# Gradient operands made inside the last attention, and all output chunks behind it in two-bank tiles

## The chip, the cores and the metric

The kernel runs on one core of one Trainium2 chip. The metric is the device time of one execution in microseconds (us); the span, which the profile uses, runs from the first to the last instruction and is about 2 us shorter.

Words used below. *PE* does the matrix products, *VectorE* (DVE), *ScalarE* (ACT) and *GpSimd* (POOL) work on elements, *SyncE* (SP) issues most DMAs. A matrix product lands in *PSUM*, where this kernel's tiles take one bank (512 columns) or two (1024); to *evacuate* is to copy PSUM into on-chip memory, from where this kernel's DMAs write it out. A *block* is a DMA of 512 KB. In the code cuts, `T` transposes a chunk of `wo`, `M` multiplies with it, and `Z` says how many zero blocks each stage gets.

## The reference

Two attention layers and two MLP layers share one set of weights (A, B, A, B) and run on a single token; the result is the output and the gradients of all inputs:

```python
x = x + A(layernorm(x)); x = x + B(layernorm(x))
x = x + A(layernorm(x)); x = x + B(layernorm(x))
out, vjp = jax.vjp(f, A_x, A_k_cache, A_v_cache, A_wq, A_wo, B_w1, B_b1, B_w2)
return (out, *vjp(grad_out))
```

A token's weight gradient is an outer product of two short vectors, but it is as large as the weight. The gradients of the K and V caches are zero except in the last 4096 of 32768 positions, so most of them is plain zeros: 112 blocks that the kernel may write at any time, and uses to keep the DMA engines busy.

## The kernel before

The backward pass ends with the attention of the first layer, called A1. Its first step multiplies the gradient with `wo`. Nine of `wo`'s 16 chunks are kept on the chip; seven (9 to 15) are loaded again into a ring of six buffers. So six loads can be issued early, and the seventh waits until the first buffer is free.

```python
def zeros(n):                       # on SyncE's queue
    for _ in range(min(n, len(zero_jobs))):
        nc.sync.dma_start(zero_jobs.pop(0), zt[:])
def bg_zeros(n, after):             # on GpSimd's queue, not before `after` is made
    ...
def attn_bwd(...):
    held = {}
    for c in range(NR, min(NO, NR + NB)):        # chunks 9..14
        held[c] = wo_load(c)                     # nc.sync.dma_start
    bg_zeros(Z["A3c" if first else "A1c"], g_bf) # 6 zero blocks
    ...
    def T(i):
        c = late[i]
        if c not in held:
            held[c] = wo_load(c)                 # chunk 15
        ...                                      # transpose, reduce
    pipe(list(range(len(late))), T, M)
    ...
    else:
        zeros(Z["A1d"])                          # 26 zero blocks
    # --- cut: do, rows_mm with V, softmax backward, dq, product with wq;
    #     six chunks of the w2 gradient are made in between (run(..)) ---
```

Everything after the pipeline of T and M needs all seven chunks. SyncE issued its DMAs in program order here: below, the zeros begin at 304.14 us, only after the seventh load, which had waited for its buffer until 303.7.

Behind the attention the remaining gradient chunks are made. A chunk takes four 512-column products; `out_banks` gives four one-bank tiles or, once the pool "pair" exists, two two-bank tiles:

```python
def out_banks():
    if "pair" in pools:
        ts = [pools["pair"].tile([P, 1024], FP32, ...) for _ in range(2)]
        ...
    bs = [psum1([P, 512], FP32, "ops") for _ in range(4)]
# --- cut ---
g0, g0b = attn_bwd(g1, g1b, "A1", sA1, False, "X0")
# --- cut: gradient row operands are made here, after the attention ---
run(1000)                                        # rest of the w2 gradient
dw_wide(lambda: R["w1"], 256, F // 2, True, out_6)
run(4)
pt.release()
pools["pair"] = ctx.enter_context(...)           # two-bank tiles from here on
```

## Time and profile before

| | before |
|---|---|
| time, median of 4 runs | 462.57 us (460.12 to 464.96) |
| profiled span | 458.9 us |
| bytes moved by DMA | 172.24 MB |
| DMA rate when it is full | 417 to 419 GB/s |

At 417 GB/s the bytes alone take 413 of the 459 us, so the kernel is for the most part bound by DMA, and what can be won is stretches in which DMA is not full. The page shows them over the whole span in 40 slices (DMA in tenths of busy time, then GB/s):

```profile
span 458.9 us, 11945 instructions
...
DMA  8999999988999999999998999999995889799997
GB/s 322 387 411 414 406 408 342 410 307 316 416 417 370 390 342 351 411 414 416 416 414 326 311 336 368 359 412 418 416 418 235 354 321 400 309 413 402 418 411 303
```

The low slices after the 30th belong to the end of the last attention and what follows. Stage by stage (stretch, its length, then busy time and instructions of PE, weight load, DVE, ACT and POOL, the share of PE's clock that was granted, the DMA share, GB/s):

```profile
core 0: us, PE busy (x) PEld busy (x) DVE busy (x) ACT busy (x) POOL busy (x), PEclk, DMA share, GB/s
345.00:350.00 5.00, 1.59 (x10) 1.02 (x11) 1.83 (x9) 0.00 (x0) 2.02 (x10) 0.50 0.81 330
350.00:355.00 5.00, 4.40 (x40) 3.77 (x38) 3.92 (x15) 2.02 (x2) 4.47 (x22) 0.50 0.25 99
360.00:365.00 5.00, 3.94 (x16) 0.77 (x13) 3.43 (x6) 3.95 (x8) 0.00 (x0) 0.50 0.69 281
375.00:380.00 5.00, 3.10 (x20) 0.70 (x20) 4.12 (x5) 4.22 (x5) 0.00 (x0) 0.50 0.71 285
390.00:395.00 5.00, 4.66 (x42) 1.33 (x40) 5.00 (x6) 4.70 (x5) 0.00 (x0) 0.70 0.43 166
400.00:440.00 40.00, 32.88 (x192) 8.51 (x192) 38.62 (x35) 37.58 (x41) 0.00 (x0) 0.50 1.02 412
```

Three holes: the row operands (345 to 355), the one-bank chunks (360 to 380), and the K blocks, where a 1 MB write needs four chunks (390 to 395). With two-bank tiles (from 400) DMA is full.

SyncE's queue in the last attention (issue time, duration of the group, what, count):

```profile
289.07 15.01 SPq L336 DMA_DIRECT2D wo_c<-in_A_wo_dram  x7
304.14 31.08 SPq L130 DMA_DIRECT2D out_dram<-zt  x26
335.32 22.52 SPq L974 DMA_DIRECT2D out_dram<-wo_b  x7
```

All seven loads come first, then 26 zeros, which take SyncE 31 us, then outputs. The chain of work that ended last (start, duration, what) shows what the seventh load meant:

```profile
303.32 0.37 PE acc L223 x8
303.76 6.69 DMA wo_c<-in_A_wo_dram
310.50 0.64 PE tps L187 x8
```

PE freed the buffer at 303.7 us, and PE went on as soon as the load landed, at 310.5. The price of a one-bank and a two-bank evacuation (group, count | busy, mean ns of one | idle before):

```profile
L146 DVE CAST K<-ops 128x1024 bf16<-128x1024 f32 x15 | 17.7, 1221 | 0.9 <-PE ops L223 0.6
L149 ACT CAST K<-ops 128x1024 bf16<-128x1024 f32 x17 | 17.0, 1012 | 1.7 <-PE ops L223 1.2
...
L146 DVE CAST so<-ops 128x512 bf16<-128x512 f32 x4 | 2.7, 689 | 1.1 <-PE ops L223 1.0
...
L149 ACT CAST so<-ops 128x512 bf16<-128x512 f32 x4 | 2.3, 586 | 0.4 <-PE ops L223 0.4
```

Twice 689 is 1378 ns against 1221, twice 586 is 1172 against 1012: each instruction carries about 160 ns that do not depend on its size.

### The profile page before, as it was taken

What the parts mean: (1) busy time and instruction counts of PE and PEld (TensorE: products, weight loads), DVE (VectorE), ACT (ScalarE), POOL (GpSimd) and SP (SyncE); (2) the same over time, 40 slices, a digit from 0 to 9 for tenths busy, and PEclk for the clock granted to TensorE, in tenths of its full rate; (3) what the DMA queues carried; (4) which work ended last, traced back from release to release, by engine and by line L of the source; (5) the groups of instructions that cost most, each with busy time, mean ns of one, the idle gap of its engine ahead of it and who ended that gap; (6) DMA issues with size and microseconds to landing.
All of it is one profiled execution on the core that took longest, in us unless ns stands there. A gap on an engine that the chain in (4) does not pass through costs nothing.

```text
span 458.9 us, 11945 instructions
## 1 busy us (share of the span) xinstructions
PE 328.7 (72%) x5080; PEld 225.6 (49%) x5080; DVE 246.9 (54%) x519; ACT 219.3 (48%) x268; POOL 61.5 (13%) x159
## 2 busy tenths in 40 slices
PE   0565755577996998877997889775885676779730
PEld 0333434566466997854895779643534111222100
DVE  3124101376332776663265755564555779999960
ACT  1122100165242886773581655351031689998940
POOL 2000000002422214142330020112006000000000
PEclk9989555596777999895697769987565555755555
DMA  8999999988999999999998999999995889799997
GB/s 322 387 411 414 406 408 342 410 307 316 416 417 370 390 342 351 411 414 416 416 414 326 311 336 368 359 412 418 416 418 235 354 321 400 309 413 402 418 411 303
DMA packets 52257, 172.24 MB, mean 375 GB/s; under 512 B 5200, under 2 KB 12396, under 8 KB 51180
## 3 DMA queue, kind: packets, MB, share of 16 engines
q1 hardware_dynamic: 39680, 126.37, 71.3%
q0 software_dynamic: 12480, 45.11, 24.5%
q8 instruction: 39, 0.64, 0.5%
q14 instruction: 14, 0.11, 0.1%
q10 hardware_dynamic: 44, 0.01, 0.0%
HBM read 72.89 MB, written 98.58 MB: 374 GB/s over the span
## 4 chain that ended last, share of the span: by engine, by line
PE 21%; issue 9%; DVE 8%; ACT 8%; DMA 7%; POOL 1%; DVEq 0%; ACTq 0%; SPq 0%; POOLq 0%
PE tps L187 6%; PE ops L223 5%; DMA w_c<-in_B_w_dram 4%; PE acc L223 4%; ACT wo_b L149 3%; DVE wq_b L146 3%; DMA wo_c<-in_A_wo_dram 3%; DVE K L146 3%; ACT st_o L149 2%; PE d L223 2%; PE tps L602 1%; PE sm L223 1%; PE rw L887 1%; ACT wo_c L149 1%; ACT w_c L603 1%
## 5 line engine op out<-in xcount | busy, mean ns | idle before, releaser
L139 POOL DMA_DIRECT2D out_dram<-zt x86 | 45.7, 535 | 43.3 <-DMA out_dram<-zt 40.7
L223 PEld LDWEIGHTS <-w_c 128*128 128x128 bf16 x1120 | 36.3, 102 | 20.9 <-DMA w_c<-in_B_w_dram 13.9
L603 ACT COPY w_c<-tps 128x1024 bf16<-128x1024 bf16 x28 | 28.3, 1012 | 25.5 <-PE tps L602 24.8
L146 DVE CAST wo_b<-ops 128x512 bf16<-128x512 f32 (+3 forms) x40 | 33.2, 878 | 9.2 <-PE ops L223 8.9
L605 DVE CUSTOM_DVE_ANT_0 scr<-w_c,gbc 128x1024 bf16<-128x1024 bf16 x28 | 34.2, 1221 | 7.2 <-DMA w_c<-in_B_w_dram 5.2
L149 ACT CAST wo_b<-ops 128x512 bf16<-128x512 f32 (+2 forms) x34 | 27.0, 870 | 16.4 <-PE ops L223 16.4
L149 ACT COPY K<-tps 128x1024 bf16<-128x1024 bf16 x19 | 18.7, 1019 | 30.9 <-PE tps L187 30.9
L223 PE MATMUL q<-wq_b,nA_pair 128*32 128x512 bf16 x128 | 14.0, 541 | 16.6 <-DMA wq_b<-in_A_wq_dram 15.1
L770 DVE CUSTOM_DVE_ANT_0 wo_c<-wo_c,gbc 128x1024 bf16<-128x1024 bf16 x14 | 16.3, 1218 | 12.4 <-DMA wo_c<-in_A_wo_dram 10.4
L602 PE MATMUL tps<-ident_bf,w_c 128*128 128x128 bf16 x224 | 22.7, 263 | 0.0
L146 DVE COPY K<-tps 128x1024 bf16<-128x1024 bf16 x13 | 8.8, 689 | 24.9 <-PE tps L187 24.9
L149 ACT COPY w_b<-tps 128x1024 bf16<-128x1024 bf16 x20 | 19.5, 1015 | 5.3 <-PE tps L187 5.2
L187 PE MATMUL tps<-ident_bf,K 128*128 128x128 bf16 x256 | 21.7, 249 | 0.0
L223 PE MATMUL ops<-Tw 2*128 2x512 bf16 x56 | 15.9, 560 | 6.5 <-ACT wo_b L149 4.1
L187 PEld LDWEIGHTS <-K 128*128 128x128 bf16 x256 | 18.4, 114 | 4.1 <-issue 4.0
L223 PE MATMUL acc<-a_pair,w_c 128*128 128x16 bf16 x448 | 16.0, 172 | 5.2 <-DMA w_c<-in_B_w_dram 4.2
L187 PE MATMUL tps<-ident_bf,w_c 128*128 128x128 bf16 x224 | 17.3, 238 | 1.6 <-DMA w_c<-in_B_w_dram 1.6
L146 DVE CAST K<-ops 128x1024 bf16<-128x1024 f32 x15 | 17.7, 1221 | 0.9 <-PE ops L223 0.6
L149 ACT CAST K<-ops 128x1024 bf16<-128x1024 f32 x17 | 17.0, 1012 | 1.7 <-PE ops L223 1.2
L149 ACT COPY w_c<-tps 128x768 bf16<-128x768 bf16 (+1 forms) x14 | 11.6, 829 | 12.6 <-PE tps L187 11.4
L149 ACT COPY wq_b<-tps 128x1024 bf16<-128x1024 bf16 x16 | 15.1, 1054 | 5.1 <-PE tps L187 5.1
L223 PE MATMUL ops<-R 2*128 2x512 bf16 (+1 forms) x64 | 12.3, 544 | 7.0 <-ACT wo_b L149 5.4
(333 smaller groups left out, 684.5 us busy)
## 6 DMA issues: line engine op xcount, KB each, us to landing
out_dram<-zt POOLq DMA_DIRECT2D x86, 512.0 KB, 10.0
wo_c<-in_A_wo_dram SPq DMA_DIRECT2D x28, 512.0 KB, 8.2
w_c<-in_B_w_dram SPq DMA_DIRECT2D x32, 448.0 KB, 5.9
w_c<-in_B_w_dram SPq DMA_DIRECT2D x28, 512.0 KB, 7.0
out_dram<-zt SPq DMA_DIRECT2D x26, 512.0 KB, 8.2
out_dram<-wo_b SPq DMA_DIRECT2D x18, 512.0 KB, 9.1
wq_b<-in_A_wq_dram SPq DMA_DIRECT2D x16, 512.0 KB, 11.8
out_dram<-K SPq DMA_DIRECT2D x8, 1024.0 KB, 8.4
```

The costliest lines, as they stand in the source:

```text
L139: nc.gpsimd.dma_start(zero_jobs.pop(0), zt[:])
L146: nc.vector.tensor_copy(out_ap, in_ap)
L149: nc.scalar.copy(out_ap, in_ap)
L187: nc.tensor.transpose(ps[:, b, :], ap, ident_bf[:])
L223: nc.tensor.matmul(out_ap, lhsT=lhsT, rhs=rhs, start=start, stop=stop, skip_group_check=True, **kw)
L602: nc.tensor.transpose(ps[:, b, :], w[:, 1, b * P:(b + 1) * P], ident_bf[:])
L603: nc.scalar.copy(w[:, 1, :], ps[:].rearrange("p b c -> p (b c)"))
L605: nc.vector.tensor_tensor_reduce(out=scr[:], in0=w[:, 0, :], in1=gbc[:], scale=1.0, scalar=0.0, op0=ALU.mult, op1=ALU.add, accum_out=wg[:, ...
L770: nc.vector.tensor_tensor_reduce(out=w[:, 0, :], in0=w[:, 0, :], in1=gbc[:], scale=1.0, scalar=0.0, op0=ALU.mult, op1=ALU.add, accum_out=w ...
L887: nc.tensor.transpose(ps[:, j, :], sp[:, j, :], ident_bf[:])
```

## The change

The intent: fill the last attention with zeros alone, use its idle engines to make all row operands, and let the outputs then leave at full DMA rate, with a zero block between every nine chunks as reserve. The diff, cut to its core:

```diff
 def attn_bwd(...):
-        bg_zeros(Z["A3c" if first else "A1c"], g_bf)
+        if first:
+            bg_zeros(Z["A3c"], g_bf)
+        else:
+            zeros(Z["A1"])              # 29 blocks, on SyncE's queue
 ...
+        if not first:
+            after_do()                  # buffers for operands, in wo's place
+            prep.extend([ ... ])        # seven operand steps
         def T(i): ...
+            if not first and i:
+                nextprep()              # at the end of M
         pipe(list(range(len(late))), T, M)
 ...
-            zeros(Z["A1d"])
+            after_stream()
 ...     # in the rest of the attention: nextprep() where run() and tall_left() were
-Z = dict(..., A3c=6, A3d=29, W1=3, A1c=6, A1d=26, end=4)
+Z = dict(..., A3c=6, A3d=29, W1=3, A1=29)
 ...     # behind the attention
-    run(1000)
-    dw_wide(lambda: R["w1"], 256, F // 2, True, out_6)
-    run(4)
     pt.release()
     pools["pair"] = ctx.enter_context(...)
 ...
+    run(6)
+    while jobs:
+        zeros(1)
+        run(9)
```

The operands moved from a pool of their own into the places of `wo` and V (cut). The bytes are the same.

## The prediction

> **What bounds the kernel now.** The DMA engines: the page lists 172.24 MB over 458.9 us, and the best stretches of the table of stages carry 417 to 419 GB/s, so the bytes alone need about 413 us. The change touches only what follows the last weight pass (about 295 us on). There the table shows holes: 345 to 355 us (330 and 99 GB/s: gradient row operands are built after the attention), 360 to 380 us (281, 376, 353, 285 GB/s: outputs leave through one-bank tiles, with VectorE and ScalarE evacuations of 128x512 at about 0.65 and 0.58 us), and 390 to 395 us (166 GB/s: K staging). Against 417 GB/s these cost about 12 us. From 400 us, with two-bank tiles (1.22 and 1.01 us for 128x1024), DMA holds about 412 GB/s.
>
> **What the change does.** It takes the output chunks out of the last attention, builds the row operands there, uses two-bank tiles for all outputs and spreads seven zero blocks over them. Two-bank evacuation gives a 512 KB chunk about every 1.1 us against 1.26 us on DMA, so the tail should be DMA-bound and all three holes should close.
>
> **What it costs.** To feed DMA in the attention it issues 29 zero blocks on SyncE's queue, right after six of the seven streamed wo loads. The instruction order shows the seventh load (last wo chunk) now *behind* all 29; before, it was ahead of the 26 and only six zeros on GpSimd's queue ran beside it. The Trainium skill, "DMA: Bandwidth & Descriptors", section "Queues, rings and completion order", says that each engine consumes a ring's descriptors in order; in this trace the 26 zeros took SyncE 31 us to issue[...]. Before, the seventh load landed at 310.5 us and the attention went on at once (6.7 us of DMA wait in the chain of waits). Now, from about 295 us, some 4.5 outstanding blocks, 29 zeros and the load itself, at 1.26 us each, put its landing at about 338 us. From it hangs the whole rest of the attention: before, 310.5 to 346.7 us, 36 us. Without output chunks I estimate 29 us, plus about 3 us for the operands that are now in line: 32 us. So the attention ends at about 370 us, and DMA, out of zeros, idles from 338 to about 373 us: one hole of 35 us for the 12 it closes.
>
> **Sum.** First output data at about 373.5 us; 39.8 MB of gradients plus seven zeros, 43.5 MB at 412 GB/s, is 105.6 us; drain 1.5 us: span about 480 us. The median before is 0.9% above its profiled span, so about **484 us, range 473 to 492**. Faster by over 2% 0.04, within 2% 0.08, slower by over 2% 0.88.
>
> **Right or wrong, in the profile.** (1) The seventh wo load issued near 330 us and landing near 338 us, the engines idle for over 20 us before it, and that DMA wait in the chain. (2) DMA near zero from about 338 to 373 us. (3) Attention remainder of about 32 us after the landing. (4) Above 405 GB/s in nearly the whole tail, no hole at K, and 128x1024 evacuations only.
>
> **What would make it wrong.** If the load overtakes the zeros, the attention ends near 345 us beside them, and the span would be about 452 us, faster by 1.5 to 2%. If the rest of the attention is much shorter (a higher granted clock; now 0.5 to 0.6 there), some 5 us less.

## The result, and the profile after

| | before | after |
|---|---|---|
| time, median of 4 runs | 462.57 us | 486.75 us (483.63 to 488.48) |
| ratio | | 1.0516 (1.0436 to 1.0595) |
| profiled span | 458.9 us | 486.7 us |
| seventh `wo` load issued / landed | 303.8 / 310.5 us | 333.0 / 342.9 us |
| gradient out of the last attention | 346.5 us | 373.9 us |

A ratio here is the mean time of one kernel's fast runs over that of the other's in the same rounds, so it is not quite the ratio of the medians. The brackets are the 95% interval.

The page, as shown above for before:

```profile
span 486.7 us, 11887 instructions
...
DMA  8999999999999999999979999999000999999997
GB/s 328 387 415 419 407 370 383 342 359 392 413 375 396 350 307 377 415 417 417 414 291 310 329 342 339 416 420 417 26 1 3 393 413 403 413 413 409 421 415 301
```

Three slices of 12 us each move almost nothing; after them all slices but the last are at 393 GB/s or more. By stage:

```profile
340.00:345.00 5.00, 2.10 (x24) 1.84 (x24) 1.23 (x2) 0.98 (x1) 0.00 (x0) 0.50 0.26 105
345.00:350.00 5.00, 2.69 (x29) 1.17 (x32) 1.89 (x10) 1.24 (x3) 0.64 (x4) 0.50 0.01 3
350.00:355.00 5.00, 3.55 (x41) 1.96 (x33) 2.68 (x10) 1.09 (x2) 0.59 (x4) 0.84 0.00 0
365.00:370.00 5.00, 3.36 (x51) 1.35 (x43) 2.18 (x12) 0.40 (x1) 1.15 (x5) 1.00 0.02 5
375.00:380.00 5.00, 3.46 (x22) 0.67 (x15) 4.55 (x4) 4.60 (x6) 0.46 (x1) 0.50 0.50 200
400.00:440.00 40.00, 32.21 (x195) 6.95 (x196) 37.28 (x34) 37.21 (x38) 0.00 (x0) 0.59 1.02 409
```

SyncE's queue names the reason:

```profile
291.46 7.82 SPq L335 DMA_DIRECT2D wo_c<-in_A_wo_dram  x6
299.33 32.66 SPq L129 DMA_DIRECT2D out_dram<-zt  x29
332.96 0.34 SPq L335 DMA_DIRECT2D wo_c<-in_A_wo_dram  x1
376.75 4.94 SPq L991 DMA_DIRECT2D out_dram<-wo_b  x5
```

Six loads, then all 29 zeros, and only then the seventh load, 29 us later than before. The load's buffer had been free since 308.8 us. The chain of work that ended last now runs through the zeros:

```profile
312.85 10.05 DMA out_dram<-zt
322.92 9.97 DMA out_dram<-zt
332.96 9.89 DMA wo_c<-in_A_wo_dram
342.90 1.05 PE tps L186 x8
```

SyncE put out the 29 zeros in 32.7 us, 1.13 us each, hardly faster than DMA moved them. Two things held it. Up to about 315 us the issue instructions themselves were long, mostly 0.9 to 1.3 us against 0.33 us later; what holds an instruction there the profile does not say. After that an issue began only when the DMA eight issues earlier had landed: the chain's 312.85, 322.92 and 332.96 are eight issues apart, and each step of 10 us is a zero on its way.

The attention computes nothing until the load lands (PE idle for 28 us, VectorE for 33 us), and by then its 29 zeros are used up. So its remaining 31 us, 342.9 to 373.9, pass with next to nothing on DMA (0 to 5 GB/s in the full windows shown).

The account closes. Counted in missing bytes at 417 GB/s, DMA lost 36 us between 340 and 380 us after, and 13 us between 345 and 395 us before: 23 us more. In the profiled execution after, the gradient reached the last attention at 300.8 us, before at 296.4; the code up to there is the same but for the place of V in memory, and in nine profiled executions with that code it varied from 294.8 to 300.8. These 4.4 us are spread between executions. Together 27.7 of the 27.8 us between the spans; the medians, with less of that spread, differ by 24.2.

### The profile page after: what moved, and what is told of

It is laid out like the page before. It is cut to its first block, busy times and chain, and to the rows that moved or that the text cites. A ratio compares the mean times of both kernels' runs of the same rounds, so it can differ in the third digit from the quotient of the medians.

```text
span 486.7 us, 11887 instructions
## 1 busy us (share of the span) xinstructions
PE 323.9 (67%) x5080; PEld 222.1 (46%) x5080; DVE 236.7 (49%) x489; ACT 225.3 (46%) x262; POOL 56.3 (12%) x145
## 4 chain that ended last, share of the span: by engine, by line
PE 18%; DMA 17%; ACT 10%; issue 4%; DVE 3%; SPq 3%; DVEq 0%; POOL 0%; ACTq 0%; POOLq 0%
PE tps L186 6%; ACT wq_b L148 5%; DMA w_c<-in_B_w_dram 4%; DMA out_dram<-zt 4%; DMA wo_c<-in_A_wo_dram 4%; PE acc L222 4%; PE ops L222 3%; SPq L129 3%; DMA out_dram<-wo_b 2%; DMA out_dram<-st_o 2%; PE d L222 1%; PE tps L602 1%; ACT st_o L148 1%; DMA out_dram<-wq_b 1%; ACT wo_b L148 1%
## 5 line engine op out<-in xcount | busy, mean ns | idle before, releaser
L138 POOL DMA_DIRECT2D out_dram<-zt x76 | 40.7, 538 | 43.1 <-DMA out_dram<-zt 40.5
L603 ACT COPY w_c<-tps 128x1024 bf16<-128x1024 bf16 x28 | 28.3, 1012 | 25.4 <-PE tps L602 14.1
L222 PE MATMUL ops<-V 2*128 2x512 bf16 (+1 forms) x160 | 34.0, 588 | 6.5 <-ACT wq_b L148 3.5
L605 DVE CUSTOM_DVE_ANT_0 scr<-w_c,gbc 128x1024 bf16<-128x1024 bf16 x28 | 34.2, 1221 | 7.3 <-DMA w_c<-in_B_w_dram 5.3
L145 DVE CAST wq_b<-ops 128x1024 bf16<-128x1024 f32 (+1 forms) x31 | 33.9, 1148 | 3.8 <-PE ops L222 3.2
L148 ACT CAST wq_b<-ops 128x1024 bf16<-128x1024 f32 (+1 forms) x33 | 33.8, 1141 | 2.2 <-PE ops L222 2.0
L222 PE MATMUL ops<-wo_b 2*128 2x512 bf16 x120 | 23.3, 567 | 10.9 <-ACT wq_b L148 7.2
L186 PE MATMUL tps<-ident_bf,wo_c 128*128 128x128 bf16 x112 | 9.1, 233 | 31.2 <-DMA wo_c<-in_A_wo_dram 31.2
L148 ACT COPY wo_c<-tps 128x1024 bf16<-128x1024 bf16 x14 | 14.0, 1026 | 30.9 <-PE tps L186 30.6
L222 PEld LDWEIGHTS <-V 128*128 128x128 bf16 (+2 forms) x416 | 14.0, 101 | 27.6 <-issue 27.6
L222 PE MATMUL q<-wq_b,nA_pair 128*32 128x512 bf16 x128 | 12.0, 461 | 18.0 <-DMA wq_b<-in_A_wq_dram 16.6
L186 PEld LDWEIGHTS <-wo_c 128*128 128x128 bf16 x112 | 7.2, 104 | 32.7 <-DMA wo_c<-in_A_wo_dram 31.5
L148 ACT COPY w_b<-tps 128x1024 bf16<-128x1024 bf16 x20 | 19.5, 1015 | 5.3 <-PE tps L186 4.9
```

Source lines behind the costliest of these rows:

```text
L138: nc.gpsimd.dma_start(zero_jobs.pop(0), zt[:])
L145: nc.vector.tensor_copy(out_ap, in_ap)
L148: nc.scalar.copy(out_ap, in_ap)
L186: nc.tensor.transpose(ps[:, b, :], ap, ident_bf[:])
L222: nc.tensor.matmul(out_ap, lhsT=lhsT, rhs=rhs, start=start, stop=stop, skip_group_check=True, **kw)
L603: nc.scalar.copy(w[:, 1, :], ps[:].rearrange("p b c -> p (b c)"))
```

## The experiments

Theory: what costs the time is the place of the seventh load in SyncE's queue. Rival 1: the new attention itself is slow, because the operands are now in it and no chunk leaves during it, whatever the order. Rival 2: the zeros fill the DMA engines, and any load would have to wait for them.

### e1: six zeros ahead of the load, 23 behind it

```diff
-            zeros(Z["A1"])
+            zeros(6)
 ...     # after the pipeline of T and M
+            zeros(23)
             after_stream()
```

> Changed kernel, but only 6 of the 29 zero blocks stand ahead of the seventh wo load and 23 behind it. Queue-order theory: the load is issued near 309 us and lands near 316 us instead of 342.9; the rest of the attention keeps its 31 us and ends near 347; first output issued near 350 and the tail keeps its 110 us: span about 460, ratio to before 0.98 to 1.01. Rival (the attention itself got slower because the row operands are now in it and no output chunk leaves during it, whatever the order of the queue): ratio stays at 1.03 or more, and the remainder of the attention, not the landing, is what is long.

Measured: 460.77 us, ratio 1.0011 (0.9952 to 1.0069). The load was issued at 306.0 and landed at 313.3 us, the gradient came at 346.9 us, the first output was issued at 349.8. The whole loss of 5% is gone, with the new attention in place: rival 1 falls. But nothing is won over before either, for one hole remains, because 29 zeros end before the attention does:

```profile
335.00:340.00 5.00, 3.46 (x51) 1.39 (x43) 2.29 (x11) 0.25 (x1) 1.16 (x5) 1.00 0.92 374
340.00:345.00 5.00, 1.91 (x12) 1.78 (x8) 0.86 (x2) 0.76 (x1) 0.00 (x0) 0.61 0.06 20
345.00:350.00 5.00, 2.39 (x15) 1.07 (x16) 2.93 (x9) 1.57 (x2) 0.52 (x1) 0.50 0.01 2
...
385.00:390.00 5.00, 4.65 (x40) 0.95 (x34) 4.21 (x4) 4.52 (x6) 0.00 (x0) 0.50 1.02 402
```

### e2: all 29 zeros ahead, but the load in another queue

```diff
-    def wo_load(c):
+    def wo_load(c, eng=None):
 ...
-        nc.sync.dma_start(w, wo_v[c])
+        (eng or nc.sync).dma_start(w, wo_v[c])
 ...     # in T
-                held[c] = wo_load(c)
+                held[c] = wo_load(c, None if first else nc.gpsimd)
```

> Changed kernel with all 29 zeros still ahead in SyncE's queue, but the seventh wo load is issued by GpSimd, so it goes into another queue. Same bytes in flight at the same time. Queue-order theory: the load is issued near 312 us (behind GpSimd's spreads) and lands within about 10 us, near 322; the span is about 486 - 21 = 465, ratio 0.99 to 1.02. Rival (bandwidth: the zeros fill the DMA engines, and any load would wait for them): it lands near 340 as before and the ratio stays near 1.05.

Measured: 461.31 us, ratio 1.0014 (0.9947 to 1.0081). Zeros and load in order of time (start, duration, engine, what):

```profile
300.01 29.70 SPq L129 DMA_DIRECT2D out_dram<-zt  x25
...
308.75 0.54 POOL L335 DMA_DIRECT2D wo_c<-in_A_wo_dram  x1 [0.33 <-DMA out_dram<-zt]
...
317.00 1.04 PE L186 MATMUL tps<-ident_bf,wo_c 128*128 128x128 bf16 x8 [5.62 <-DMA wo_c<-in_A_wo_dram]
```

SyncE was still issuing zeros until 329.7 us, and DMA moved 414 GB/s from 310 to 320 us. Yet the load landed 8.2 us after its issue, and did not wait for 17 zeros that had stood ahead of it in program order (12 of the 29 were out when the load was issued). Rival 2 falls: with DMA full, the load did not have to wait until the zeros were done.

The times also say which wait it was. Counted from the moment at which the gradient entered the attention, the load landed after 19.5 us here and after 42.1 us in the changed kernel. Of these 22.6 us, 20.9 lie in the issue, and only 1.7 between issue and landing (8.2 against 9.9 us). So the load was held by SyncE, which had its zeros to issue first, and hardly by data that stood ahead of it in the DMA engines. That it also shared the engines with zeros already in flight agrees with the Trainium skill, "DMA: Bandwidth & Descriptors", section "Queues, rings and completion order", which says that each DMA engine takes turns between the queue rows that have work: from 314 to 315 us the trace has 0.22 MB on the load's queue and 0.21 MB on SyncE's. My expectation of 465 us was too high, since the load was issued 3 us and landed 5 us earlier than I had put it.

### e3: fifteen zeros ahead, 14 behind

The same edit as e1, with 15 and 14.

> Changed kernel with 15 zeros ahead of the seventh wo load and 14 behind it. Queue-order theory, one block at 1.26 us: landing 14 x 1.26 = 17.6 us earlier than 342.9, so near 325; span near 469, ratio about 1.01 to 1.02, between e1 and the change. Rival (the attention itself): ratio near 1.05.

Measured: 467.02 us, ratio 1.0158 (1.0100 to 1.0215). The chain of work that ended last:

```profile
304.07 8.56 DMA out_dram<-zt
312.71 9.83 DMA wo_c<-in_A_wo_dram
322.59 1.05 PE tps L186 x8
```

To compare the runs, I count the landing from the moment at which the gradient entered the attention:

| run | zeros ahead of the load in its queue | load landed after | attention still took |
|---|---|---|---|
| e1 | 6 | 15.3 us | 33.6 us |
| e3 | 15 | 24.9 us | 31.0 us |
| changed kernel | 29 | 42.1 us | 31.0 us |
| e4 | 32 | 46.1 us | 38.1 us (with output chunks) |

From e3 to the changed kernel it is 17.2 us for 14 blocks, 1.23 us each; the full DMA rate gives 1.26. But the first zeros cost nothing. PE was done with the load's buffer at 305.9 us in e1, 305.7 in e3, 308.8 in the changed kernel and 305.0 in e4, and the load was issued 0.1, 7.0, 24.2 and 27.8 us after that. In e1 SyncE had issued its six zeros by 303.5 us, before the buffer was free. So in these runs only the zeros that SyncE had still to issue when the buffer came free delayed the load.

### e4: the kernel before, with its zeros ahead of the load

```diff
-        bg_zeros(Z["A3c" if first else "A1c"], g_bf)
+        if first:
+            bg_zeros(Z["A3c"], g_bf)
+        else:
+            zeros(Z["A1c"] + Z["A1d"])   # 32
 ...
-        else:
-            zeros(Z["A1d"])
```

> Kernel before, and only the order changed: all its 32 zeros of the last attention go on SyncE's queue ahead of the seventh wo load; chunks, one-bank tiles and operands as before. Queue-order theory: the load lands near 342 to 346 us instead of 310.5, the attention follows it, and the span grows by 26 to 34 us: ratio 1.055 to 1.075. Rival (what slows the changed kernel is the new attention): ratio within 1.00 to 1.01.

Besides the order, six of the 32 zeros change from GpSimd's queue to SyncE's.

Measured: 494.70 us, ratio 1.0747 (1.0689 to 1.0806), at the upper end of what was expected. The same wait appears in the kernel before:

```profile
323.20 9.53 DMA out_dram<-zt
332.80 9.88 DMA wo_c<-in_A_wo_dram
342.72 1.05 PE tps L187 x8
```

So zeros ahead of the load suffice for the loss, without anything else of the change, and e1 shows that with only six ahead there is none. It costs more here than in the changed kernel (7.5% against 5.2%). That fits the better tail of the changed kernel, of which e6 and e7 measure a part.

### e5 and e9: seven more zeros under the attention

In e1 DMA is dry for about 10 us while seven zeros wait in a tail that is full anyway. e5 moves them: `zeros(6)` ahead of the load, `zeros(30)` behind it, none left for the tail.

> As e1 (6 zeros ahead of the seventh load), but the seven zeros that were spread over the output tail are also written during the attention, 30 behind the load. In e1 DMA ran dry at about 340.5 us and the first output data came at about 350.5: a hole of 10 us; seven more blocks at 1.26 us cover 8.8 of it, and the tail has 3.7 MB less. If DMA bytes are all that is left to bound this part, the span falls by about 8 us against e1, to about 452, ratio to before 0.975 to 0.985. If the spread zeros were needed (K staging without them leaves DMA dry), a hole of 3 us or more shows at the first K blocks and the gain is 4 to 5 us (ratio about 0.99).

> The same kernel as e5, for comparing with e8 on the same chip: ratio to before within 0.974 to 0.985.

Measured: 452.92 us, ratio 0.9795 (0.9745 to 0.9844), and in other rounds, as e9, 453.50 us, ratio 0.9824 (0.9773 to 0.9875). This is the fastest kernel, faster than both given ones; whether it passes the mark of 2% is not settled by these intervals. The gain over e1 is 8 us by the medians and 2.2% (10 us) by the ratios, which come from different rounds; the seven blocks are worth 8.8 us. A part of the second branch is there too: without the spread zeros DMA runs short at the K blocks, where e1 had 402 GB/s:

```profile
345.00:350.00 5.00, 2.69 (x16) 0.67 (x16) 3.58 (x9) 2.39 (x3) 0.52 (x1) 0.50 0.47 190
...
385.00:390.00 5.00, 4.67 (x37) 0.93 (x32) 4.04 (x4) 4.47 (x6) 0.00 (x0) 0.50 0.60 242
```

These are 2.7 and 2.1 us of missing bytes. The zeros between the chunks do their work, but the same zeros are worth more in the attention.

### e6 and e7: the two-bank tiles

e6 is e5 without the pool of two-bank tiles:

```diff
-    pt.release()
-    pools["pair"] = ctx.enter_context(...)
```

> e5 with the two-bank tiles taken away: all outputs through the four one-bank tiles, evacuations of 128x512. If the two-bank tiles are what keeps the tail at DMA speed, the tail drops to the 330 GB/s or so that the kernel before shows at 360 to 380 us: 39.8 MB then take about 120 us instead of 97, ratio to before 1.01 to 1.04. If they don't matter, it stays within 1% of e5.

Measured: 477.61 us, ratio 1.0330 (1.0269 to 1.0391), so 5.5% slower than e5 (1.0330 / 0.9795). The diff is cut: `pt.release()` moves to the end. e7 is the kernel before with the switch to two-bank tiles moved ahead of the rest of the w2 and of the w1 gradient:

```diff
+    pt.release()
+    pools["pair"] = ctx.enter_context(...)
     run(1000)
     dw_wide(lambda: R["w1"], 256, F // 2, True, out_6)
-    run(4)
-    pt.release()
-    pools["pair"] = ctx.enter_context(...)
```

> Kernel before, and only the switch to two-bank tiles moved ahead: it happens right after the last attention, not after four chunks of the w1 gradient. If the one-bank chunks cost what the holes at 360 to 380 us show (4.5 us of missing DMA at 417 GB/s, with those of 355 to 360 us), the span falls by 3 to 6 us, ratio 0.987 to 0.994. If the time is set elsewhere (outputs wait for DMA anyway), ratio 0.997 to 1.003.

Measured: 457.32 us, ratio 0.9893 (0.9847 to 0.9939; one of six runs was slow and is not in the ratio): 5 us, as expected. So this part of the change was good by itself. Why: a chunk of 512 KB needs 1.26 us on DMA. By an estimate from the evacuation times above, two-bank tiles empty it in 1.11 us with VectorE and ScalarE side by side (1/(1/1221+1/1012) = 553 ns per half), and one-bank tiles in 1.27 us at best (1/(1/689+1/586) = 317 ns per quarter), before any wait. Against DMA's 1.26 us that is about 1 us over all 78 chunks, but e6 lost 25. In e6 the one-bank tiles also use only four banks, so one chunk is in flight where the two-bank pool holds two. How the loss divides between the two I did not test.

### e8: four zeros borrowed from the first backward attention

```diff
-    Z = dict(..., A3d=29, W1=3, A1=29)
+    Z = dict(..., A3d=25, W1=3, A1=29)
-            zeros(Z["A1"])
+            zeros(6)
 ...
+            zeros(32)
```

> As e5, but four zeros are moved from the first backward attention (A3, about 195 to 245 us, 29 to 25 there) to the end: 6 ahead of the seventh load, 32 behind it, two again in the output tail before the K blocks. In e5 DMA stands part idle at 345 to 350 us (190 GB/s, 2.7 us of bytes missing) and at 385 to 390 us (242 GB/s, 2.1 us). If the first backward attention is bound by its DMA bytes (417 GB/s throughout), it gets 4 x 1.26 = 5 us shorter, these two holes close, and the span falls by 3 to 5 us against e5: ratio to before about 0.97. If that attention needs its zeros as cover just as the last one does, a hole of the same size opens near 240 to 250 us and the ratio stays at 0.977 to 0.983.

Measured: 456.41 us, ratio 0.9894 (0.9842 to 0.9946), against 0.9824 for e5's kernel in the same rounds. No gain, but rather a loss (the two intervals still overlap), and above both ranges that I had given:

```profile
245.00:250.00 5.00, 2.75 (x43) 2.68 (x44) 3.11 (x10) 0.00 (x0) 0.00 (x0) 0.74 0.48 192
250.00:255.00 5.00, 5.00 (x133) 4.46 (x130) 4.87 (x8) 4.29 (x5) 0.00 (x0) 0.92 0.48 137
...
385.00:390.00 5.00, 4.89 (x32) 0.91 (x32) 4.85 (x5) 4.43 (x5) 0.00 (x0) 0.50 1.02 396
```

The hole at the K blocks closed (396 GB/s); the one at the first output chunks stayed (241 GB/s from 350 to 355 us); and one opened behind the first backward attention, where e5's profile has 387 and 326 GB/s. In missing bytes at 417 GB/s these ten us cost 6.1 us, and 1.5 in e5. That attention took 53.7 us with 25 zeros and 54.4 us with 29 (in e9): it looked bound by DMA, at 417 GB/s throughout, and by these two executions it is not. The zeros there were its cover, as they are in the last one. There is a fixed stock of them, and I tried no other place.

## Why the prediction was right

The time was forecast as 484 us (473 to 492); it is 486.75. Point by point:

1. *The seventh load.* Predicted issue near 330, landing near 338 us; measured 333.0 and 342.9. Of the 4.9 us by which it was late, 4.4 are the later start of the attention in that execution. e1, e2 and e4 show that this is the cause: fewer zeros ahead or another issuing engine, no loss; zeros ahead in the kernel before, the full loss. The prediction names two reasons side by side, the order within a ring and the pace at which SyncE issues. The second carries it: the load was issued 24.2 us after its buffer was free, and then took 9.9 us to land, where it had taken 6.7 before. Its reason for that pace is cut: in the trace before, the DMA eight issues earlier had landed 0.9 us or more before each zero's issue, as far as the trace tells, and it was the issue itself that lasted 1.0 to 1.6 us.
2. *DMA near zero from 338 to 373 us.* It was, from about 341 to 377 us.
3. *32 us of attention behind the landing.* 31.0 us. The two estimates in it (29 without chunks, 3 for operands) were not tested one by one.
4. *The tail.* Predicted 107 us from the first data; measured 109.9 us from the first issue at 376.75 to the end. The rate from 400 to 440 us was 409 GB/s where I had put 412, and no hole shows at the K blocks. "Above 405 GB/s in nearly the whole tail" was a little too high: two of the 5 us stretches from 380 to 425 us have 401 and 404.
5. *From span to time.* I added 0.9% because the median before lay that far above its span. The step in the profiled runs is about 2 us in both kernels; the rest of my 4 us was spread between runs, and by chance it made up for part of a span put 7 us too low.

The sum of the holes was right in kind: one of 36 us for 13 us closed. The evacuation prices are near those of the Trainium skill, "VectorE: DVE Perf Modes", section "The TRN2 errata — SBUF-src ops pay a fixed extra latency per instruction", whose formula for PSUM to SBUF gives 1192 and 658 ns on VectorE for 1024 and 512 columns (120 cycles and one per column at 0.96 GHz): the trace has 1221 and 689 ns, some 30 ns more.

## What to carry to other kernels

Put filler traffic behind every load that the critical path still needs, not only behind those that can be issued now, or let another engine issue the load. In this kernel a load that waited for a buffer was delayed by the filler that SyncE had still to issue ahead of it when the buffer came free: six blocks cost nothing, and each of the sixteenth to the 29th cost 1.23 us; issued by GpSimd, the same load did not wait for them. A fixed stock of filler was worth most where the compute chain is long and DMA would be dry (e5); and a stage that shows a full DMA rate may be full only because of the filler (e8).

## What the Trainium skill lacked or had wrong

- "DMA: Bandwidth & Descriptors", section "Issuing engines are not separate DMA queues", says that issuing from several engines will only save the sequencer's time to start a DMA, and that this is usually small beside the DMA itself. No run here contradicts the first part, but the time was not small: in the changed kernel SyncE took 32.7 us to issue 29 blocks. In e2 one load gained 20.9 us in its issue, and then landed in 8.2 us, and the kernel went from 5.2% slower than the kernel before to 0.1%.
- The same page, section "Queues, rings and completion order", states the order and the turns, but no page draws the practical rule: what an engine has still to issue ahead of a late load, when that load could go, delays it by its full transfer time (17.2 us for 14 blocks of 512 KB between e3 and the changed kernel; nothing for the six of e1, which were out before).
- "VectorE: DVE Perf Modes": the formula for PSUM sources is some 30 ns short per instruction here (1221 and 689 ns against 1192 and 658).
